# Key-feature gradient made transposed, 512 columns at a time, with its rows turned back by DMA

## The chip, the cores and the metric

The kernel runs on one core of a Trainium2 chip. The metric is the device time of one execution in microseconds (us). The kernel before has a median of 820.01 us over three runs (819.78 to 821.04).

The engines are called as the profile calls them: PE is the matrix engine (PEld its weight loads), DVE the vector engine, ACT the scalar engine, POOL the GpSimd engine, SP the sync engine, which here only issues DMAs. A matmul multiplies a stationary 128x128 operand (`lhsT`) with a moving operand of up to 512 columns and accumulates in PSUM, which has eight banks of 512 f32 values in each of 128 partitions. DVE and ACT bring results from PSUM to SBUF.

## The reference

The reference computes the output and all gradients of one transformer block: a layer norm, a linear attention with 32 heads of 20, a residual, a second layer norm, a gated MLP, a residual. Sizes: S = 2048 rows, D = 640, F = 1728, all in bf16. The part that matters here, cut:

```python
qkv = (x @ wqkv) ...                       # x is the normalised input, here xn
phi = lambda t: jnp.where(t > 0, t + 1, jnp.exp(t)) + 1e-6
pq, pk = phi(q), phi(k)
kv = jnp.einsum("bhsd,bhse->bhde", pk, v)
z = jnp.einsum("bhsd->bhd", pk)
num = jnp.einsum("bhqd,bhde->bhqe", pq, kv)
den = jnp.einsum("bhqd,bhd->bhq", pq, z)[..., None] + 1e-6
o = num / den
...
_out, _vjp = jax.vjp(_f, A_x, A_wqkv, A_wo, B_w1, B_w3, B_w2)
```

Backward through the key features: the gradient of `pk` is `xn @ gm + gz`, where `gm` (640x640) is the value weight times the gradient of `kv`, and `gz` (640 numbers) is the gradient of `z`. The gradient before the nonlinearity is `g_k = min(pk, 1) * (xn @ gm + gz)`. From it come the key part of the weight gradient, `xn^T @ g_k`, and, with `g_q` and `pk`, the gradient of `xn`: `[g_q, g_k, pk] @ wqT`, where `wqT` stacks the turned query weight, key weight and `gm`.

## The kernel before

The kernel is one program with its order written out by hand: each engine executes its instructions in the order of the source, waits are put in by the framework. It runs in stages: forward attention, forward and backward MLP, MLP weight gradients, the gradient of the second layer norm with the query side of the attention (`b_ghn`, `b_gr`, `b_gq`), then the stages that the change touches, then the big MLP weight gradients (`grad_job` over `blocks`, line 1335).

Rows are held as `[128 partitions, 16 tiles, 640]`, tile `t` being rows 128t to 128t+127. A turned tensor has the 640 features on partitions (five blocks of 128) and rows along the free side; `xnT[c]` holds 512 rows of turned `xn` (c = 0 to 3).

What the steps of the change and of the prediction touch, in order of time:

- **Last parts of the query side** (from line 1239). `part()` emits a piece of `q_parts` (line 1219), the matmuls that read `r_sb` and `g_h`. As each of its five outputs is complete, ACT copies it and SP turns it by DMA (line 1226, `QT`). In the same stretch SP issues the loads that turn `xn` (`load_xnT`, line 1242) and the weights (`load_wqT`, line 1299).
- **Jobs.** `wq_jobs` makes the weight gradients of q or k, in ten jobs (five blocks of 128 by two halves of 320 columns); a job is 16 matmuls of 320 columns into a PSUM tile of one bank (line 1335), one ACT copy to a place of `obs` (line 1339) and a DMA out (line 1341; POOL's queue for q, SP's for k). `fill(n)` emits n half jobs: it is how PE gets independent work between dependent pieces. `obs` holds 3200 columns, ten places of 320, which the jobs use in turn.
- **Squares.** `square` (line 1369) makes 128 rows of a 640x640 product into a tile of `d_acc`, which is `[128, 2, 512]` f32, two banks; there are three such tiles. Columns 0 to 379 lie in the first bank, 380 to 639 in the second. `unload` (line 1375) lets ACT copy the first bank's part and DVE the second's. Five squares make `dwoT`, five make `gm`, five make the value weight gradient, which also goes by way of `obs`: its five row blocks use columns 2560 on, then 0, 640, 1280 and 1920.
- **The key gradient** (loop from line 1436). A broadcast of `gz` over partitions is made first (lines 1426 to 1434). For each tile of 128 rows ten matmuls of 320 columns (line 1442) put `xn @ gm` into both banks of a `d_acc` tile; DVE adds `gz` (line 1445) and multiplies with `min(pk, 1)` (line 1446), `pk` rows being loaded by `load_pk`. After odd tiles below 13 comes `fill(1)`, after every third tile a square of the value gradient. All ten matmuls of a tile are issued before DVE reads the tile.
- **The gradient of x** (loop from line 1520). `e_gxn` issues 30 matmuls of 320 columns per tile (line 1505): five turned blocks of `g_q` and five of `g_k`, both brought by `e_T` (line 1498, a DMA transpose of 128x640), and five of the turned `pk` (`pkT`, loaded at line 1464). Then `ln_bwd` runs on ACT and DVE (lines 1143 to 1156), and SP writes the row tile out (line 1527). Twelve half jobs of the key weight gradient stand before the loop and two before every third tile of it. In the same loop SP loads the inputs of the last stage: `hnN` (line 1490) and the first blocks of the MLP gradients (line 1482).

The lines with which all this is ordered:

```python
def d_acc():
    return ps.tile([P, 2, 512], F32, name="dkv", bufs=3)
...
def unload(acc, out):
    for bank, (a, b) in enumerate(((0, SPLIT_D), (SPLIT_D, H))):
        (A.copy, V.tensor_copy)[bank](out=out[:, a * DH:b * DH], in_=acc[:, bank, 0:(b - a) * DH])
...
def fill(n):
    for _ in range(n):
        next(jobs, None)
```

An earlier product (`f2_wT`, lines 705 and 708) has the same shape as a square and the same split between ACT and DVE, but takes two PSUM tiles of one bank each.

Of the kernel before, what the change touches and what calls it, by code (L numbers as in the profile page):

```python
# [9 lines left out]
P = 128  # L10
BF16 = mybir.dt.bfloat16
F32 = mybir.dt.float32
ALU = mybir.AluOpType
# [42 lines left out]
def kernel(  # L56
# [19 lines left out]
    V, A, T, G, SY = nc.vector, nc.scalar, nc.tensor, nc.gpsimd, nc.sync  # L76
# [54 lines left out]
    class Stats:  # L131
# [150 lines left out]
    def two(ap):  # L282
        return ap.rearrange("p (j n) -> p j n", j=2)
# [1014 lines left out]
    def load_wqT(k):  # L1298
        dmaT(out=wqT[:, k * DT:(k + 1) * DT, :], in_=A_wqkv[:, k * D:(k + 1) * D])
# [11 lines left out]
    part(3)  # L1311
    load_xnT(1)
    part(4)
    part(4)
    part(20)
    load_xnT(2)
    V.reduce_sum(out=gz[:], in_=gz8[:], axis=AX.X)


# [42 lines left out]
    def d_acc():  # L1362
        return ps.tile([P, 2, 512], F32, name="dkv", bufs=3)

    def square(lhsT, rhs, i):

        acc = d_acc()
        for c, a, b, bank, off, first in SQ:
            T.matmul(acc[:, bank, off:off + (b - a) * DH], lhsT=lhsT[:, c, i * P:(i + 1) * P],  # L1369
                     rhs=rhs[:, c, a * DH:b * DH], start=first, stop=True, skip_group_check=True)  # L1370
        return acc
# [20 lines left out]
        if i > 1:  # L1392
            fill(1)
    br.release()
    bo.release()
    bv = pool("bv")
    pkT = bv.tile([P, DT, S], BF16, name="pkT")
    small = bv.tile([P, ST, D], BF16, name="small", tag="hnN")
    mN, gkv_b, gm = (small[:, n:n + DT] for n in (0, DT, 2 * DT))
    gzd = small[:, 3 * DT, :].rearrange("p (m q) -> p m q", q=P)  # L1400
    dx = pool("dx", "right")

    def load_pk(c):
        pkb[c] = dx.tile([P, 2, D], BF16, name="pkb", bufs=4)
        (dma if c < 4 else dmaG)(out=pkb[c][:], in_=pk_v[:, c * 2:(c + 1) * 2, :])

    gzb = dx.tile([P, D], F32, name="gzb")
    g_k = gqkv[1] = U1.tile([P, ST, D], BF16, name="g_k", tag="S0")
    load_pk(0)
    load_pk(1)  # L1410
    dma(out=mN, in_=m_v)
    dma(out=rows(dwoT_d), in_=dwoT[:])
    load_pk(2)
    load_pk(3)
    load_xnT(3)
    load_wqT(0)

    for i, (c, ms) in enumerate(SQ_BLOCKS):
        unload(square(wqT[:, 2 * DT:, :], gkvT, i), gm[:, i, :])
# [5 lines left out]
        if i == 0:  # L1425
            for m in range(DT):
                V.tensor_scalar(out=gzd[:, m, :], in0=ident[:], scalar1=gz[:, m:m + 1], scalar2=None, op0=ALU.mult)
        dmaT(out=wqT[:, 2 * DT:, i * P:(i + 1) * P], in_=gm[:, i, :])
    acc = d_acc()
    for m in range(DT):  # L1430
        T.matmul(acc[:, m // 4, m % 4 * P:(m % 4 + 1) * P], lhsT=ones[:], rhs=gzd[:, m, :], start=(m % 4 == 0),
                 stop=True, skip_group_check=True)
    for x, y, bank in ((0, 4 * P, 0), (4 * P, D, 1)):
        A.copy(out=gzb[:, x:y], in_=acc[:, bank, 0:y - x])

    for t in range(ST):
        c, i = divmod(t, TPC)
        u = t // 2
        acc = d_acc()
        for j in range(2):  # L1440
            for k in range(DT):
                T.matmul(acc[:, j, 0:HD], lhsT=xnT[c][:, k, i * P:(i + 1) * P], rhs=gm[:, k, j * HD:(j + 1) * HD],  # L1442
                         start=(k == 0), stop=(k == DT - 1))
        gp = dx.tile([P, D], F32, name="gp")
        V.tensor_tensor(out=two(gp[:]), in0=acc[:, :, 0:HD], in1=two(gzb[:]), op=ALU.add)
        V.scalar_tensor_tensor(out=g_k[:, t, :], in0=pkb[u][:, t % 2, :], scalar=1.0, in1=gp[:], op0=ALU.min,
                               op1=ALU.mult)
        if t % 2 and t < 13:
            fill(1)

        if t in (2, 5, 8, 11, 14):
            n = t // 3
            acc = square(mN, gkv_b, n)
            k = (4, 0, 1, 2, 3)[n]
            ob = obs[:, k * D:(k + 1) * D]
            unload(acc, ob)
            dmaG(out=out2S[:, n, 2 * D:3 * D], in_=ob)
        if t % 2 and u + 4 < 8:
            load_pk(u + 4)
        if t == 2:  # L1460
            load_wqT(1)
        if t in (6, 8, 10, 12):
            n = t // 2 - 3
            dmaT(out=pkT[:, :, n * W:(n + 1) * W], in_=pk_d[n * W:(n + 1) * W, :])
    for _ in jobs:
        pass
    dx.release()
# [1 line left out]


    ex = pool("ex", "right")
    hnN = bv.tile([P, ST, D], BF16, name="hnN")
    blocks = [(f0, min(f0 + NB, 2 * F)) for f0 in range(0, 2 * F, NB)]
    NB0 = 160

# [16 lines left out]
    gT = {}  # L1492

    def e_T(t, k):
        if k == 0:
            gT[t] = (ex.tile([P, 2 * DT, P], BF16, name="gT") if t % 3 == 2 else
                     bd[:, 2 * (t % 3):2 * (t % 3) + 2, :].rearrange("p c (k q) -> p (c k) q", q=P))
        dmaT(out=gT[t][:, k * DT:(k + 1) * DT, :], in_=gqkv[k][:, t, :])

    def e_gxn(t):  # L1500
        acc = ps.tile([P, 2, 512], F32, name="gxn", tag="gxn", bufs=2)
        for j in range(2):
            for k in range(15):
                g = gT[t][:, k, :] if k < 2 * DT else pkT[:, k - 2 * DT, t * P:(t + 1) * P]
                T.matmul(acc[:, j, 0:HD], lhsT=g, rhs=wqT[:, k, j * HD:(j + 1) * HD], start=(k == 0),  # L1505
                         stop=(k == 14))
        gx = scr[:, t % 2, :]
        ln_bwd(acc, t, xnN[:, t, :], ln1, gx, g_h[:, t, :], ex, scr[:, 2 + t % 2, :], scr[:, 4, :])()
        return gx
# [3 lines left out]
    njob = 2  # L1513
    jobs = wq_jobs((1,))
    scr = U1.tile([P, DT, D], BF16, name="scr", tag="W6")
    for t in range(3):
        for k in range(2):
            fill(2)
            e_T(t, k)
    for t in range(ST):  # L1520
        if t > 1 and t % 3 == 0:
            fill(2)
        gx = e_gxn(t)
        if t + 3 < ST:
            for k in range(2):
                e_T(t + 3, k)
        dma(out=out1S[:, t, :], in_=gx)
        if t in (2, 3, 5, 6):
            load_hnN((2, 3, 5, 6).index(t))
        if t in (7, 9, 12):  # L1530
            load_block(0, (t - 7) // 2 * NB0, (t - 5) // 2 * NB0 if t < 12 else NB)
        if t == 13:
            load_block(1)
    for _ in jobs:
        pass

# [32 lines left out]
            gw2_turn(i)  # L1569
    ps.release()  # L1570
    ex.release()
    bv.release()
    bl.release()
    U1.release()
# [31 lines left out]
```

## Time and profile before

| what | value |
|---|---|
| median of three runs | 820.01 us (819.78 to 821.04) |
| the profiled execution | 819.99 us; its span, first to last instruction, 817.9 us |
| PE | busy 811.8 us, 99% of the span |
| DVE, ACT, POOL | 55%, 40% and 16% |
| mean granted clock of PE | 1.000 |
| 560.7 to 579.1 us | half jobs, `dwoT`, `gm` |
| 579.1 to 609.5 us | the key gradient, with half jobs and squares |
| 609.5 to 624.7 us | rest of the query jobs, first key jobs |
| 624.7 to 698.6 us | the gradient of x, with the rest of the key jobs |
| 698.6 to 815.2 us | the MLP weight gradients |

Times in the profile are us from the start of the span unless marked ns. A group of instructions is given as line, engine, operation, output<-inputs, shape and count, then its busy time and the mean ns of one, then the idle time of its engine just ahead of it and what ended that. A matmul's shown duration is longer than its share of the stream: 30 matmuls of 512 columns in a row take 6.47 us, while each is shown with 379 ns.

### The profile page before, as it was taken

What the parts mean: (1) busy time and instruction counts of PE and PEld (TensorE: products, weight loads), DVE (VectorE), ACT (ScalarE), POOL (GpSimd) and SP (SyncE); (2) the same over time, 40 slices, a digit from 0 to 9 for tenths busy, and PEclk for the clock granted to TensorE, in tenths of its full rate; (3) what the DMA queues carried; (4) which work ended last, traced back from release to release, by engine and by line L of the source; (5) the groups of instructions that cost most, each with busy time, mean ns of one, the idle gap of its engine ahead of it and who ended that gap; (6) DMA issues with size and microseconds to landing.
All of it is one profiled execution on the core that took longest, in us unless ns stands there. A gap on an engine that the chain in (4) does not pass through costs nothing.

```text
span 817.9 us, 13715 instructions
## 1 busy us (share of the span) xinstructions
PE 811.8 (99%) x5261; PEld 501.6 (61%) x5292; DVE 452.7 (55%) x973; ACT 324.8 (40%) x609; POOL 131.8 (16%) x198
## 2 busy tenths in 40 slices
PE   9999999999999999999999999999999999999998
PEld 6777544555555555754577777777777777544444
DVE  7859997998898566300057777772781544200000
ACT  7856688665565666011222212222212334211111
POOL 2243333333222212100001111110220000000000
PEclk9999999999999999999999999999999999999999
DMA  9799899696485556999967877266997888979991
GB/s 268 201 243 287 198 270 319 196 242 174 126 211 157 165 175 168 230 238 243 260 176 182 214 198 196 58 113 142 252 206 158 182 193 158 240 179 233 218 242 37
DMA packets 335761, 162.46 MB, mean 199 GB/s; under 512 B 252304, under 2 KB 328944, under 8 KB 335696
## 3 DMA queue, kind: packets, MB, share of 16 engines
q1 hardware_dynamic: 291936, 120.68, 63.9%
q0 software_dynamic: 7328, 24.48, 9.2%
q10 hardware_dynamic: 36432, 16.42, 8.0%
q8 instruction: 41, 0.67, 0.4%
q14 instruction: 24, 0.20, 0.1%
HBM read 47.09 MB, written 53.43 MB: 123 GB/s over the span
## 4 chain that ended last, share of the span: by engine, by line
PE 98%; ACT 1%; DVE 1%; issue 0%; POOL 0%; ACTq 0%
PE mm L395 20%; PE job L1335 20%; PE ghn L1131 14%; PE gxn L1505 8%; PE gw L1086 7%; PE big L268 4%; PE o L913 4%; PE o L859 3%; PE gwo L1219 3%; PE macc L430 3%; PE gr L1188 3%; PE dkv L1442 3%; PE at L657 2%; PE mm L268 1%; PE dkv L1369 1%; PE gp L395 1%
## 5 line engine op out<-in xcount | busy, mean ns | idle before, releaser
L1335 PE MATMUL job<-gb,hnN 128*128 128x496 bf16 (+3 forms) x576 | 116.8, 366 | 0.0
L1131 PEld LDWEIGHTS <-ggb 128*128 128x128 bf16 x864 | 84.5, 98 | 33.0
L395 PE MATMUL mm<-pqT,w 128*128 128x512 bf16 x396 | 93.2, 379 | 0.5
L1335 PEld LDWEIGHTS <-hnN 128*128 128x128 bf16 x576 | 55.7, 98 | 61.1
L395 PEld LDWEIGHTS <-w 128*128 128x128 bf16 x540 | 52.5, 98 | 63.2 <-issue 0.6
L1339 ACT CAST obs<-job 128x496 bf16<-128x496 f32 (+4 forms) x56 | 28.5, 509 | 123.7 <-PE job L1335 123.7
L1131 PE MATMUL ghn<-w13a,ggb 128*128 128x320 bf16 x448 | 63.5, 299 | 0.0
L1146 DVE SCALAR_TENSOR_TENSOR wb<-gs,hnb 128x640 f32<-128x640 bf16 x16 | 13.2, 825 | 88.1 <-ACT gs L1143 88.1
L1131 PE MATMUL ghn<-w13b,ggb 128*128 128x320 bf16 x416 | 61.4, 299 | 0.0
L395 PE MATMUL mm<-g2T,w2T 128*128 128x512 bf16 x228 | 58.9, 379 | 0.6
L1086 PE MATMUL gw<-hb,g 128*128 128x512 bf16 (+2 forms) x316 | 58.4, 345 | 0.2
L1086 PEld LDWEIGHTS <-g 128*128 128x128 bf16 x320 | 31.3, 98 | 27.0
L420 ACT CAST ghh<-mm 128x512 bf16<-128x512 f32 x48 | 28.1, 585 | 47.6 <-PE mm L395 41.2
L1196 POOL TENSOR_TENSOR sz<-Zb,g_h 128x640 f32<-128x640 bf16 x16 | 20.2, 1261 | 163.8 <-DVE g_h L1197 163.8
L796 ACT ACTIVATE sig<-mm 128x512 bf16<-128x512 f32 x56 | 33.7, 602 | 25.5 <-PE mm L395 21.7
L1143 ACT ACTIVATE gs<-ghn 128x640 bf16<-128x640 f32 x16 | 11.2, 703 | 75.9 <-PE ghn L1131 66.1
L395 PEld LDWEIGHTS <-w2T 128*128 128x128 bf16 x260 | 25.4, 98 | 23.4
L268 PEld LDWEIGHTS <-pqT 128*128 128x128 bf16 x320 | 30.8, 98 | 13.4 <-ACT pqT L260 1.3
L268 PE MATMUL big<-wqkv,pqT 128*128 128x320 bf16 x250 | 38.4, 299 | 0.3
L1335 PEld LDWEIGHTS <-g 128*128 128x128 bf16 x320 | 31.0, 98 | 11.6
L832 DVE TENSOR_TENSOR gate<-gate,sig 128x1024 bf16<-128x1024 bf16 x28 | 19.3, 690 | 33.8 <-ACT gate L807 31.0
L1091 ACT CAST gw2o<-gw 128x512 bf16<-128x512 f32 (+2 forms) x20 | 10.4, 519 | 66.7 <-PE gw L1086 25.6
(217 smaller groups left out, 1391.8 us busy)
## 6 DMA issues: line engine op xcount, KB each, us to landing
hh_d<-hhT SPq DMA_DIRECT2D x24, 256.0 KB, 2.7
gg_d<-gate POOLq DMA_DIRECT2D x24, 256.0 KB, 4.2
gg_d<-ghh POOLq DMA_DIRECT2D x24, 256.0 KB, 3.9
ggb<-gg_d SPq DMA_DIRECT2D x6, 896.0 KB, 5.3
ggb<-gg_d ACTq DMA_DIRECT2D x6, 832.0 KB, 5.4
ggb<-gg_d SPq DMA_DIRECT2D x2, 1728.0 KB, 12.6
x_sb<-in_A_x_dram SPq DMA_DIRECT2D x4, 640.0 KB, 4.7
pk_d<-pk_all SPq DMA_DIRECT2D x4, 640.0 KB, 5.3
```

Of the source, the lines that this page charges most:

```text
L268: T.matmul(acc, lhsT=pqT[:, c, t * P:(t + 1) * P], rhs=wqkv[:, c, n0:n0 + HD], start=(c == 0), stop=(c == DT - 1))
L395: T.matmul(acc[:], lhsT=w[:, c, fc * P:(fc + 1) * P], rhs=rhs[:, c, :], start=(c == 0), stop=(c == DT - 1))
L420: A.copy(out=ghh[n // 2][:, n % 2, :], in_=acc[:])
L430: T.matmul(macc[m][j][:, 0:n], lhsT=pk_all[:, t, m * P:(m + 1) * P], rhs=x_ext[:, t, j * HD:j * HD + n], start=(t == 0), stop=(t == ST - 1))
L796: A.activation(sig[:, i, :], gp[:], AF.Sigmoid)
L859: T.matmul(accs[i, j][:, 0:HD], lhsT=hhT[c][:, fc, i * P:(i + 1) * P], rhs=w2[:, fc, j * HD:(j + 1) * HD], start=(first and fc == 0), stop ...
L913: T.matmul(o2["ps"][:, 0:HD], lhsT=hhT[c][:, fc, i * P:(i + 1) * P], rhs=w2[:, fc, j * HD:(j + 1) * HD], start=(fc == 0), stop=(fc == FT - 1))
L1086: T.matmul(acc[:, 0:fw], lhsT=g2[:, t, m * P:(m + 1) * P], rhs=hb[b][:, t, 0:fw], start=(t == 0), stop=(t == ST - 1))
L1131: T.matmul(acc[:, j, 0:HD], lhsT=ggb[t // 2][:, k, lo:lo + P], rhs=rhs[:, j * HD:(j + 1) * HD], start=(k == 0), stop=(k == NG - 1))
L1335: T.matmul(acc[:, 0:n], lhsT=lhs[:, t, m * P:(m + 1) * P], rhs=rhs(t), start=(t == 0), stop=(t == ST - 1))
L1339: A.copy(out=ob, in_=acc[:, 0:n])
L1505: T.matmul(acc[:, j, 0:HD], lhsT=g, rhs=wqT[:, k, j * HD:(j + 1) * HD], start=(k == 0), stop=(k == 14))
```

## The change

The key gradient is made turned. Instead of 16 row tiles of ten 320-column matmuls there are 20 pieces: for each of the four groups of 512 rows and each of the five blocks of 128 features, five matmuls with 512 moving columns. Within a group of 512 rows the pieces for feature blocks 0 and 1 share one `d_acc` tile, block 0 in its first bank and block 1 in its second, likewise blocks 2 and 3; block 4 has a tile of its own. Numbered through from 0 to 19, the pieces 1, 3, 6, 8, 11, 13, 16 and 18 are second halves of a tile. After each piece DVE makes `pm = min(pkT, 1)` (128x512, in SBUF), and then `g_kT = (piece + gz) * pm`, reading the piece's bank; `gz` is now a number per partition, so its broadcast goes. A half job follows each odd-numbered piece below 16, and a square of the value gradient the odd-numbered pieces 9 to 17.

`pkT` is needed for this and is loaded earlier, its first half into the room of `r_sb`; the loads of `pk` rows go. `e_gxn` takes the key part directly from `g_kT`, so `e_T` only turns `g_q`, five tiles ahead. The rows of `g_k`, which the key weight gradient needs, are brought by 20 DMA transposes of 128x512 (`k_turn`) during the gradient of x, and all ten key jobs stand behind that loop. `hnN` takes the room of `g_q` and is loaded at tiles 11 to 14, the first block at 11, 13 and 15, the second block after the loop. `load_wqT(0)` moves into the query side's last parts, `load_xnT(2)` behind the store of `dwoT`, the load of `mN` behind the turning of `gm`.

```diff
     load_xnT(1)
     part(4)
+    load_wqT(0)
     part(4)
     part(20)
-    load_xnT(2)
+    bo.release()
+    bv = pool("bv")
+    pkT = bv.tile([P, DT, S], BF16, name="pkT")
+
+    def load_pkT(c):
+        dmaT(out=pkT[:, :, c * W:(c + 1) * W], in_=pk_d[c * W:(c + 1) * W, :])
+
+    load_pkT(0)
+    load_pkT(1)
...
-    load_pk(0)
-    load_pk(1)
-    dma(out=mN, in_=m_v)
     dma(out=rows(dwoT_d), in_=dwoT[:])
-    load_pk(2)
-    load_pk(3)
-    load_xnT(3)
-    load_wqT(0)
+    load_xnT(2)
...
+    gT = {}
+
+    def e_T(t):
+        gT[t] = bd[:, t % DT, :].rearrange("p (k q) -> p k q", q=P)
+        dmaT(out=gT[t], in_=g_q[:, t, :])
+
+    mN = U1.tile([P, DT, D], BF16, name="mN", tag="W6")
+    load_pkT(2)
+    dma(out=mN[:], in_=m_v)
+    load_xnT(3)
+    load_pkT(3)
+    load_wqT(1)
+
+    for n in range(SC * DT):
+        c, d = divmod(n, DT)
+        cs = slice(c * W, (c + 1) * W)
+        if d % 2 == 0:
+            acc = d_acc()
+        for k in range(DT):
+            T.matmul(acc[:, d % 2, :], lhsT=gm[:, k, d * P:(d + 1) * P], rhs=xnT[c][:, k, :], start=(k == 0),
+                     stop=(k == DT - 1))
+        pm = dx.tile([P, W], BF16, name="pm", bufs=2)
+        V.tensor_scalar(out=pm[:], in0=pkT[:, d, cs], scalar1=1.0, scalar2=None, op0=ALU.min)
+        V.scalar_tensor_tensor(out=g_kT[:, d, cs], in0=acc[:, d % 2, :], scalar=gz[:, d:d + 1], in1=pm[:], op0=ALU.add,
                                op1=ALU.mult)
-        if t % 2 and t < 13:
+        if n % 2 and n < 16:
             fill(1)
+        if n > 8 and n % 2:
+            i = (n - 9) // 2
+            if i < DT:
+                sq = square(mN, gkv_b, i)
+                k = (4, 0, 1, 2, 3)[i]
+                ob = obs[:, k * D:(k + 1) * D]
+                unload(sq, ob)
+                dmaG(out=out2S[:, i, 2 * D:3 * D], in_=ob)
+    for t in range(DT):
+        e_T(t)
...
-    hnN = bv.tile([P, ST, D], BF16, name="hnN")
+    hnN = g_q
...
+    def k_turn(n):
+        c, d = divmod(n, DT)
+        dmaT(out=g_k[:, c * TPC:(c + 1) * TPC, d * P:(d + 1) * P], in_=g_kT[:, d, c * W:(c + 1) * W])
...
-                g = gT[t][:, k, :] if k < 2 * DT else pkT[:, k - 2 * DT, t * P:(t + 1) * P]
+                ts = slice(t * P, (t + 1) * P)
+                g = gT[t][:, k, :] if k < DT else g_kT[:, k - DT, ts] if k < 2 * DT else pkT[:, k - 2 * DT, ts]
...
-    for t in range(3):
-        for k in range(2):
-            fill(2)
-            e_T(t, k)
     for t in range(ST):
-        if t > 1 and t % 3 == 0:
-            fill(2)
         gx = e_gxn(t)
-        if t + 3 < ST:
-            for k in range(2):
-                e_T(t + 3, k)
+        if t + DT < ST:
+            e_T(t + DT)
+        for n in (2 * t, 2 * t + 1):
+            if n < SC * DT:
+                k_turn(n)
         dma(out=out1S[:, t, :], in_=gx)
-        if t in (2, 3, 5, 6):
-            load_hnN((2, 3, 5, 6).index(t))
...
+        if t > 10 and t < 15:
+            load_hnN(t - 11)
...
+    load_block(1)
     for _ in jobs:
         pass
```

More of the change, by code (lines that the diff above doesn't have):

```diff
@@ L1394 @@
     br.release()
[L1395 to L1407, printed above, removed]
+    bs = pool("bs")
+    g_kT = bs.tile([P, DT, S], BF16, name="g_kT")
+    dx = pool("dx")
+    gm, gkv_b = (dx.tile([P, DT, D], BF16, name=n) for n in ("gm", "gkv_b"))
     g_k = gqkv[1] = U1.tile([P, ST, D], BF16, name="g_k", tag="S0")
-    load_pk(0)
-    load_pk(1)
-    dma(out=mN, in_=m_v)
     dma(out=rows(dwoT_d), in_=dwoT[:])
-    load_pk(2)
-    load_pk(3)
-    load_xnT(3)
-    load_wqT(0)
+    load_xnT(2)
     for i, (c, ms) in enumerate(SQ_BLOCKS):
@@ L1424 @@
         fill(1)
-        if i == 0:
-            for m in range(DT):
-                V.tensor_scalar(out=gzd[:, m, :], in0=ident[:], scalar1=gz[:, m:m + 1], scalar2=None, op0=ALU.mult)
         dmaT(out=wqT[:, 2 * DT:, i * P:(i + 1) * P], in_=gm[:, i, :])
[L1429 to L1446, printed above, removed]
+    gT = {}
@@ L1447 @@
                                op1=ALU.mult)
-        if t % 2 and t < 13:
+        if n % 2 and n < 16:
             fill(1)
[L1451 to L1464, printed above, removed]
+        if n > 8 and n % 2:
[6 more added lines that the diff above has]
+                dmaG(out=out2S[:, i, 2 * D:3 * D], in_=ob)
@@ L1490, in load_hnN @@
         dma(out=hnN[:, i * TPC:(i + 1) * TPC, :], in_=hn_v[:, i * TPC:(i + 1) * TPC, :])
[L1492 to L1498, printed above, removed]
+    def k_turn(n):
+        c, d = divmod(n, DT)
+        dmaT(out=g_k[:, c * TPC:(c + 1) * TPC, d * P:(d + 1) * P], in_=g_kT[:, d, c * W:(c + 1) * W])
     def e_gxn(t):
@@ L1515 @@
     scr = U1.tile([P, DT, D], BF16, name="scr", tag="W6")
-    for t in range(3):
-        for k in range(2):
-            fill(2)
-            e_T(t, k)
     for t in range(ST):
-        if t > 1 and t % 3 == 0:
-            fill(2)
         gx = e_gxn(t)
-        if t + 3 < ST:
-            for k in range(2):
-                e_T(t + 3, k)
-        dma(out=out1S[:, t, :], in_=gx)
-        if t in (2, 3, 5, 6):
-            load_hnN((2, 3, 5, 6).index(t))
[L1530 to L1533, printed above, removed]
+        if t + DT < ST:
[3 more added lines that the diff above has]
+                k_turn(n)
+        dma(out=out1S[:, t, :], in_=gx)
+        if t > 10 and t < 15:
+            load_hnN(t - 11)
+        if t in (11, 13, 15):
+            load_block(0, (t - 11) // 2 * NB0, (t - 9) // 2 * NB0 if t < 15 else NB)
+    load_block(1)
     for _ in jobs:
@@ L1571 @@
     ex.release()
+    bs.release()
     bv.release()
```

## The prediction

> **What bounds the kernel now.** I read the page's engine line first, then the chain of waits, then the table by stage, then the instructions around the places that the change edits. The engine line and the table (busy time and count of PE, PEld, DVE, ACT and POOL, then clock, DMA share, GB/s; the four rows are the stages named above):
>
> ```profile
> PE 811.8 (99%) x5261; PEld 501.6 (61%) x5292; DVE 452.7 (55%) x973; ACT 324.8 (40%) x609; POOL 131.8 (16%) x198
> ...
> 560.70:579.14 18.44, 18.44 (x194) 14.83 (x193) 7.93 (x27) 7.09 (x16) 2.77 (x5) 1.00 0.81 224
> 579.14:609.50 30.36, 30.36 (x247) 22.41 (x245) 25.20 (x34) 4.64 (x11) 7.30 (x12) 1.00 1.19 208
> 609.50:624.70 15.20, 15.20 (x114) 10.94 (x113) 2.75 (x5) 2.55 (x6) 1.08 (x2) 1.00 0.91 192
> 624.70:698.60 73.90, 73.90 (x546) 53.16 (x544) 35.73 (x90) 27.38 (x50) 0.00 (x0) 1.00 0.83 172
> ```
>
> In every stage that the change touches PE is busy for the whole stage, at full clock. So nothing can be won by shortening a wait; only PE work taken away gains, and every new PE wait costs its full length. The chain, in order of time (start, length, what), with matmul counts:
>
> ```profile
> 6.46 0.98 PE k L268 x5
> ...
> 290.72 6.47 PE mm L395 x30
> ...
> 579.30 0.28 PE dkv L1431 x5
> 579.58 2.72 PE dkv L1442 x20
> 582.30 1.09 PE job L1335 x8
> ```
>
> It gives the prices on PE: 2.72/20 = 0.136 us for 320 columns, 6.47/30 = 0.216 for 512, 1.09 for a half job.
>
> The last view is what decides. A square fills two banks of one PSUM tile, ACT reads the first bank, DVE the second (timeline, then who waited, for line 1375; below it the same for line 708, where the banks are two tiles):
>
> ```profile
> 571.33 0.49 PE L1369 MATMUL dkv<-bd,wqT 128*128 128x140 bf16 x6
> ...
> 571.90 0.47 ACT L1375 CAST small<-dkv 128x380 bf16<-128x380 f32 x1 [0.99 <-PE dkv L1369]
> 572.41 0.43 DVE L1375 CAST small<-dkv 128x260 bf16<-128x260 f32 x1 [1.03 <-ACT small L1375]
> ...
>   DVE small L1375: 3.7, 4
>   DVE dwoT L1375: 2.4, 3
> ```
> ```profile
> 79.61 0.83 PE L705 MATMUL wt<-bd,wo 128*128 128x140 bf16 x12
> ...
> 79.99 0.91 ACT L708 CAST pkx<-wt 128x380 bf16<-128x380 f32 x2
> 80.14 0.76 DVE L708 CAST pkx<-wt 128x260 bf16<-128x260 f32 x2 [0.33 <-PE wt L705]
> ```
>
> With one tile DVE starts at 572.41, just after ACT ends (571.90 + 0.47), though it reads the other bank; and ACT starts only after the last of the six matmuls (571.33 + 0.49 = 571.82), though the last ones write the other bank. With two tiles ACT and DVE run side by side, and ACT starts at 79.99 while the matmuls into the other tile still run. So engines are ordered by tile, not by bank.
>
> **The change part by part.** *PE work.* Out: 160 matmuls of 320 columns, 160 x 0.136 = 21.76 us, and the broadcast of gz, 0.28. In: 100 of 512 columns, 100 x 0.216 = 21.57. Sum -0.47 us. Half jobs, squares and the 480 matmuls of the gradient of x keep count and shape.
>
> *The shared tile.* Within a tile the second piece's matmuls now stand behind DVE's read of the first. By the rows above PE must wait for that read. One wait: DVE starts 0.20 after a tile's stream ends (583.22 + 1.36 = 584.58; the add at line 1445 starts 584.78); the read of 512 columns is 0.69, on the line between the 260-column cast (0.428) and the 640-column operation at 1446 (0.825), bounds 0.48 (the 320-column add at line 664) and 0.825; PE restarts 0.05 after DVE ends (line 161 ends 95.76, PE 95.81). Together 0.94 (0.73 to 1.08). There are eight second pieces. Before 6, 8 and 16 a half job of 1.09 stands between and covers it: 0, and about 0.9 each if that cover were gone. Before 1, 3, 11, 13 nothing does: 4 x 0.94 = 3.8. Before 18 a square (0.34) covers a part, but DVE also has that square's second half to copy: 0.7. Before 11, DVE's half of a square (ACT 0.24 after it, 0.475, then DVE 0.42) and `pm` (0.33, from 0.378 for 640 columns at line 299) make the read 0.2 late, and 0.2 more falls on a square waiting for its tile at the end. Sum 4.9 (3.7 to 6.2).
>
> *obs.* The first value square goes to columns 2560 on, where query job 8 also writes. Before, that copy came long after the square's DMA; now it is due two pieces later. From the square's end: halves copied after 1.2, POOL's issue at 1.4, landing 5.0 later (line 1457: 3.3/5.0/6.8), so 6.4; the copy is due after pieces 10 and 11, two reads and a half job, at 4.6. ACT waits 1.8; behind it in its queue is the next square's first half, behind that DVE's second half, `pm` and the read of piece 12, and behind that PE at piece 13. 2.0 with the extra handoffs; 0.3 at 3.3, 5.3 at the slowest landing of that queue in this stretch (8.3). I take 2.0, from the row of the same DMA.
>
> *DVE, ACT, LN.* `pm` and reads are 20 x (0.33 + 0.69) = 20.4 us against 26.4 of lines 1445 and 1446; beyond the waits above, PE covers it. The layer norm backward now runs 16 tiles without pauses. ACT is idle 0.29 before line 1143 in each 4.08 us tile where no job stands between (690.49, 694.56), so it keeps pace: 0.
>
> *SP's queue.* `load_wqT(0)` stands before the last two turns of qp. Its issue takes 3.7 to 6.9 (line 1299), from 556.4, so the last turn is issued at 562.5 to 565.7 instead of 561.4 + 1.2 and lands 1.4 later; it is wanted at 565.8, covered by four half jobs: 0 (0 to 1.3). Then two `pkT` loads (3.6 each) to 570, dwoT's store at 571.4, `xnT(2)` to 576, five turns of gm (1.34 each, line 1428) to 583, `pkT(2)` to 586.5, `mN` landing 5.3 later at 592; the first value square wants it at 597: 0, 5 us to spare. `xnT(3)`, `pkT(3)`, `wqT(1)` (5.5) follow to 600, five `e_T` of 1.21 to 607; the gradient of x wants the first at 618: 0. The 2.6 MB of pk rows leave this stretch, four of those loads from POOL's queue. In the gradient of x SP issues per tile one `e_T` (1.21), two `k_turn` (4/5 of it each, bound 1.98 from line 1428) and a store (0.5), 3.6 (5.7) in 4.08; `e_T` is four tiles (16 us) ahead, which the bound of 1.6 per tile over ten tiles just uses up: 0. `hnN` and the blocks are issued later, but 20 half jobs (21.8) now follow the loop and cover them (landing 5 to 10): 0. The key jobs' stores wait behind the second block's 7.5 us issue; obs has ten places: 0.
>
> Sum: -0.47 + 4.9 + 2.0 = +6.4. On the profiled execution's 819.99, which is the median of 820.01 to 0.02, that is 826.4 us. Bounds: -0.47 + 3.7 + 0.3 = +3.5 and -0.47 + 6.2 + 5.3 + 1.3 = +12.3.
>
> **The rivals.** *Not slower: the second piece doesn't wait.* Place: pieces 1, 3, 11, 13, 18. If a matmul into the second bank is not ordered against a read of the first, 4.9 goes, and three tiles in turn hide most of the ACT wait; that leaves 0.7 to 1.8 at 5.0 landing and 0 at 4: 820.2, within the noise (changes under 0.2%, 1.64 us, can't be told from none here). It decides whether a read of a first piece and matmuls of its second overlap in time. For it: no row shows PE itself waiting this way. Against: both kinds of order above, ACT behind PE and DVE behind ACT across banks. The Trainium skill, "PSUM — Partial Sum Buffer", section "PSUM bank collisions raise a hardware error", says that accesses of two engines collide only within one bank and that different banks run clean; by that rule alone the chip needs no such wait and this rival would hold, while the rows show the order kept anyway.
>
> *PE's clock falls.* The loop would be the first place with idle PE time in it: 0.7 to 3 us, every few us. If the clock were halved for half of its 32 us of matmuls, +16: 842. Against: the granted clock is 1.00 in all stages, but none of them has such gaps. The Trainium skill, "TensorE: Matmul & The Clock Gate", section "A second HAM failure mode: psum-queue depth-cycling", says that short idles between groups of 512-column matmuls made the clock oscillate between half and full; no run here shows it.
>
> *Transfers late.* `xnT(3)` took 8.35 to issue in the old crowd instead of 3.6; if two loads ahead of `mN` do so, it lands 4 us late and PE stands at the first value square: 830.
>
> **How the numbers follow.** Forecast 0.78, between its bounds 823.5 and 832.3. No wait 0.14 (faster 0.02, same 0.08, slower 0.04). Clock 0.03. Late transfers 0.05. Faster 0.02, same 0.08, slower 0.90. The range 821 to 830.5 leaves out the low side of the no-wait case, the clock, and the far ends of the forecast, under 2 in 10.
>
> **What the profile after would show.** In the loop PE is idle about 7 us, ended by DVE's write of g_kT, in four waits near 0.94 and one near 3; none before pieces 6, 8, 16. ACT waits for an obs DMA near piece 11. The stage from 579 ends near 618. The gradient of x has no PE idle time, nor has the last stage. Wrong if PE is dense through the loop, if the idle time is ended by a DMA, or if the clock is below 1.00.

## The result and the profile after

The changed kernel takes 824.86 us (median of six runs, 824.38 to 826.14), beside 820.11 us for the kernel before on the same chip: a ratio of 1.0057, 95% interval 1.0046 to 1.0068. It is slower by 4.75 us. The forecast was 826.4 us, in a range of 821.0 to 830.5.

The engine line of the page, and the table by stage with the places where the stages now end (busy time and count of PE, PEld, DVE, ACT and POOL, then clock, DMA share, GB/s):

```profile
PE 813.5 (99%) x5227; PEld 495.8 (60%) x5227; DVE 445.0 (54%) x976; ACT 324.4 (39%) x607; POOL 128.7 (16%) x194
```
```profile
560.50:579.13 18.63, 18.63 (x196) 14.99 (x194) 7.11 (x22) 7.10 (x16) 2.76 (x5) 1.00 1.03 207
579.13:616.52 37.39, 32.73 (x196) 17.69 (x194) 20.41 (x45) 4.31 (x10) 5.40 (x10) 1.00 0.80 171
616.52:682.00 65.48, 65.48 (x484) 47.17 (x483) 36.48 (x92) 25.73 (x46) 0.00 (x0) 1.00 0.60 129
682.00:704.00 22.00, 22.00 (x163) 15.75 (x161) 2.56 (x7) 5.69 (x13) 0.00 (x0) 1.00 1.14 261
704.00:823.00 119.00, 116.26 (x575) 55.38 (x572) 0.00 (x0) 20.19 (x37) 0.00 (x0) 1.00 0.72 178
```

One stage has idle PE time that it didn't have: the new loop, 37.39 us of which PE is busy 32.73. The other stages of the change are full, at full clock. The engine line hides it: its busy share is still 99%, and its busy sum even rose by 1.7 us although there is less work. Of this rise 1.6 us lie between 20 us and the first half job (538.64 before, 540.26 after), where the two programs are equal and the trace of the kernel before shows 30 matmuls fewer (3446 and 3476): records that are missing. From the first half job to the last matmul's start the busy sum rises by 0.37 us (254.52 and 254.89), because the shown end of a matmul stream is modelled and each of the five broken streams carries a tail of 0.16 (five matmuls are shown with 1.24 us and are followed after 1.08). Work is therefore read from starts. Dense, the loop would take 31.9 us: 100 matmuls at 0.215, eight half jobs at 1.09, five squares at 0.34. It takes 5.5 us longer.

The list of PE's waits between 555 and 705 us (total, count, longest), and PE's timeline through the loop (start, length, what; in brackets the idle time ahead of it and what ended it):

```profile
PE dkv L1440 <- DVE g_kT L1444: 4.7, 5, 1.3
```
```profile
579.13 1.24 PE L1440 MATMUL dkv<-xnT,gm 128*128 128x512 bf16 x5
581.22 1.24 PE L1440 MATMUL dkv<-xnT,gm 128*128 128x512 bf16 x5 [0.84 <-DVE g_kT L1444]
582.29 1.25 PE L1344 MATMUL job<-g_q,g 128*128 128x320 bf16 x8
583.38 1.24 PE L1440 MATMUL dkv<-xnT,gm 128*128 128x512 bf16 x5
585.46 1.24 PE L1440 MATMUL dkv<-xnT,gm 128*128 128x512 bf16 x5 [0.84 <-DVE g_kT L1444]
...
597.69 1.24 PE L1440 MATMUL dkv<-xnT,gm 128*128 128x512 bf16 x5
599.93 1.24 PE L1440 MATMUL dkv<-xnT,gm 128*128 128x512 bf16 x5 [1.00 <-DVE g_kT L1444]
...
602.43 1.24 PE L1440 MATMUL dkv<-xnT,gm 128*128 128x512 bf16 x5
605.00 1.24 PE L1440 MATMUL dkv<-xnT,gm 128*128 128x512 bf16 x5 [1.33 <-DVE g_kT L1444]
...
613.23 0.49 PE L1378 MATMUL dkv<-gkv_b,mN 128*128 128x140 bf16 x6
614.37 2.32 PE L1440 MATMUL dkv<-xnT,gm 128*128 128x512 bf16 x10 [0.65 <-DVE g_kT L1444]
```

There are five waits, all ended by DVE's write of `g_kT`, at the second pieces 1, 3, 11, 13 and 18, and none at 6, 8 and 16, where a half job stands between. From start to start they lose 1.01, 1.00, 1.16, 1.49 and 0.80 us (first: 581.22 - 579.13 = 2.09, less the 1.08 of five matmuls), 5.46 in all; the list shows 4.7, since each shown wait begins only behind a tail of 0.16. The order around the first of them, on both engines:

```profile
579.13 1.24 PE L1440 MATMUL dkv<-xnT,gm 128*128 128x512 bf16 x5
...
580.41 0.75 DVE L1444 SCALAR_TENSOR_TENSOR g_kT<-dkv,gz,pm 128x512 bf16<-128x512 f32 x1 [0.95 <-PE dkv L1440]
...
581.22 1.24 PE L1440 MATMUL dkv<-xnT,gm 128*128 128x512 bf16 x5 [0.84 <-DVE g_kT L1444]
```

DVE starts 0.20 after the stream ends (579.13 + 1.08 = 580.21), reads for 0.75, and PE starts 0.06 after that, in the other bank of the same tile.

The longest wait, before piece 13, contains the obs conflict. The timeline of POOL, ACT and DVE from the first value square's store on:

```profile
599.12 0.54 POOL L1455 DMA_DIRECT2D out_dram<-obs  x1 [3.55 <-DVE pm L1443]
...
602.63 0.42 ACT L1348 CAST obs<-job 128x320 bf16<-128x320 f32 x1 [4.26 <-PE dkv L1378]
602.95 0.48 ACT L1384 CAST obs<-dkv 128x380 bf16<-128x380 f32 x1
...
603.46 0.43 DVE L1384 CAST obs<-dkv 128x260 bf16<-128x260 f32 x1 [1.50 <-ACT obs L1384]
603.81 0.28 DVE L1443 TENSOR_SCALAR pm<-pkT 128x512 bf16<-128x512 bf16 x1
...
604.20 0.75 DVE L1444 SCALAR_TENSOR_TENSOR g_kT<-dkv,gz,pm 128x512 bf16<-128x512 f32 x1
```

The store was issued at 599.12 and landed at 602.53. Query job 8's copy was due 0.2 after the job's matmuls end (602.10), at 602.30, and starts at 602.63. So ACT waited 0.33, and the chain behind it (the square's first half, its second half, `pm`, the read of piece 12) is late by as much. The profile puts the end of this wait down to PE's square at line 1378, which the job's copy doesn't read and whose shown end (602.10 + 0.49) lies close to the landing; the run with other places in `obs`, below, shows that the copy starts 0.20 after its job when the store isn't in its way.

The whole difference in the profile, from the first half job (560.50 before, 560.49 after) to the last matmul's start (815.02 and 820.04), is +5.03 us: 5.46 of waits less 0.43 of PE work.

### The profile page after: what moved, and what is told of

Read it like the earlier page. It is cut to its first block, busy times and chain, and to the rows that moved or that the text cites. A ratio compares the mean times of both kernels' runs of the same rounds, so it can differ in the third digit from the quotient of the medians.

```text
span 823.0 us, 13581 instructions
## 1 busy us (share of the span) xinstructions
PE 813.5 (99%) x5227; PEld 495.8 (60%) x5227; DVE 445.0 (54%) x976; ACT 324.4 (39%) x607; POOL 128.7 (16%) x194
## 4 chain that ended last, share of the span: by engine, by line
PE 96%; DVE 1%; ACT 1%; DMA 1%; SPq 0%; issue 0%; POOL 0%; DVEq 0%; ACTq 0%
PE mm L395 20%; PE job L1344 19%; PE ghn L1131 14%; PE gxn L1495 8%; PE gw L1086 7%; PE big L268 4%; PE o L913 4%; PE o L859 3%; PE gwo L1219 3%; PE macc L430 3%; PE gr L1188 3%; PE dkv L1440 2%; PE at L657 2%; PE mm L268 1%; DMA wqkv<-in_A_wqkv_dram 1%; PE dkv L1378 1%
## 5 line engine op out<-in xcount | busy, mean ns | idle before, releaser
L1344 PE MATMUL job<-gb,g_q 128*128 128x496 bf16 (+3 forms) x576 | 116.8, 366 | 0.0
L1344 PEld LDWEIGHTS <-g_q 128*128 128x128 bf16 x576 | 55.8, 98 | 61.0
L1146 DVE SCALAR_TENSOR_TENSOR wb<-gs,hnb 128x640 f32<-128x640 bf16 x16 | 13.2, 825 | 88.1 <-ACT gs L1143 88.1
```

The costliest lines, as they stand in the source:

```text
L1344: T.matmul(acc[:, 0:n], lhsT=lhs[:, t, m * P:(m + 1) * P], rhs=rhs(t), start=(t == 0), stop=(t == ST - 1))
```

## The experiments

### Is a tile the unit of order? The kernel before, with its reads split

Two edits of the kernel *before*, whose loop has no wait. Both split DVE's addition of `gz` into its two banks. The first issues the read of the first bank ahead of the second bank's matmuls, the second behind them; the rest is equal.

```diff
+        gp = dx.tile([P, D], F32, name="gp")
         for j in range(2):
             for k in range(DT):
                 T.matmul(acc[:, j, 0:HD], ...)
-        gp = dx.tile([P, D], F32, name="gp")
-        V.tensor_tensor(out=two(gp[:]), in0=acc[:, :, 0:HD], in1=two(gzb[:]), op=ALU.add)
+            V.tensor_tensor(out=gp[:, j * HD:(j + 1) * HD], in0=acc[:, j, 0:HD], in1=gzb[:, j * HD:(j + 1) * HD], op=ALU.add)
```

> The kernel before, whose key gradient takes both banks of one tile per 128 rows. DVE's addition of gz is cut into two halves of 320 columns, and the half for the first bank is issued ahead of the matmuls into the second bank. Theory (engines are ordered by tile): PE waits in each of the 16 tiles for the first half's read, 0.20 + 0.48 + 0.05 = 0.73 us, +11.7 us: 832 (830 to 834). Rival (ordered by bank, or no order of PE behind a read): 820 to 822, for DVE's additional 16 x 0.14 us of work.

Measured: 838.61 us, ratio 1.0218 (1.0202 to 1.0235). The list of waits, and the timeline of the first tile:

```profile
PE dkv L1443 <- DVE gp L1445: 16.3, 16, 1.4
```
```profile
579.25 0.84 PE L1443 MATMUL dkv<-small,xnT 128*128 128x320 bf16 x5
580.20 0.49 DVE L1445 TENSOR_TENSOR gp<-dkv,gzb 128x320 f32<-128x320 f32 x1 [1.09 <-PE dkv L1443]
580.74 1.52 PE L1443 MATMUL dkv<-small,xnT 128*128 128x320 bf16 x10 [0.65 <-DVE gp L1445]
```

Sixteen tiles, sixteen waits. The cost is larger than expected, since the waits are not all of the first one's size: where no half job stands between two tiles, DVE is still at the tile before (second half 0.49, multiply 0.82) when the first half could be read, and the wait grows from 0.65 to as much as 1.43.

The control, with both reads behind both banks' matmuls:

```diff
-        V.tensor_tensor(out=two(gp[:]), in0=acc[:, :, 0:HD], in1=two(gzb[:]), op=ALU.add)
+        for j in range(2):
+            V.tensor_tensor(out=gp[:, j * HD:(j + 1) * HD], in0=acc[:, j, 0:HD], in1=gzb[:, j * HD:(j + 1) * HD], op=ALU.add)
```

> Control of the run with the read inside: the same two halves of 320 columns, both issued behind the matmuls of both banks. All theories: no PE wait of this kind; 820 to 822 for DVE's additional 2.2 us of work, which makes DVE about as long as PE in this loop (30.7 against 30.0 us). Only the order of the source differs between the two runs.

Measured: 819.77 us, ratio 0.9985 (0.9964 to 1.0005), no PE wait in the loop. So neither the split nor the added instruction costs; the place of the read in the program does. A matmul into one bank waits for an earlier-issued read of the other bank of its tile.

### The changed kernel with a tile for every piece

```diff
-        if d % 2 == 0:
-            acc = d_acc()
+        acc = ps.tile([P, W], F32, name="gkT", tag="dkv", bufs=3)
...
-            T.matmul(acc[:, d % 2, :], ...)
+            T.matmul(acc[:], ...)
...
-        V.scalar_tensor_tensor(out=g_kT[:, d, cs], in0=acc[:, d % 2, :], ...)
+        V.scalar_tensor_tensor(out=g_kT[:, d, cs], in0=acc[:], ...)
```

> The changed kernel, with a PSUM tile of its own for each of the 20 pieces (three buffers as before, the same matmuls, reads, half jobs and squares in the same order). Theory (a piece's matmuls wait because the read of the piece ahead is in the same tile): the five PE waits of the loop (5.5 us) go, the loop over pieces shrinks from 37.4 to about 32.0 us, and the time is that of the kernel before less the matmul overhead, 819.6 (819.3 to 820.6). Rival (the waits come from DVE being slow, from the number of buffers, or from the 512-column form): the waits stay, 824 to 825; with three one-bank buffers instead of three two-bank ones a lack of buffers would even lengthen them. It also prices all the other parts of the change together, since they are all kept: if the time is 819.6 they cost nothing.

Measured: 822.18 us, ratio 1.0024 (1.0013 to 1.0035). All five waits are gone, and 2.7 us of the loss; but two other waits came, and the expectation of 819.6 (to 820.6) was missed by 2.6. The list of waits, and the timeline around them (ACT, then PE):

```profile
PE dkv L1378 <- DVE obs L1384: 1.1, 1, 1.1
PE gkT L1439 <- DVE g_kT L1443: 0.6, 1, 0.6
```
```profile
602.66 0.43 ACT L1348 CAST obs<-job 128x320 bf16<-128x320 f32 x1 [6.04 <-DMA out_dram<-obs]
...
603.98 0.49 PE L1378 MATMUL dkv<-gkv_b,mN 128*128 128x140 bf16 x6 [1.05 <-DVE obs L1384]
```

Here ACT does stand for a long time at the first square's store (issued 597.38, landed 602.57): the loop runs ahead by what the tiles no longer cost, so job 8's copy is due earlier while the store lands at the same moment. The reason seemed to be the obs conflict; the other possible one was that three tiles of one bank hold less than three of two. The next pair tells these apart.

### The obs conflict alone

The value squares go to the places 0, 1, 2, 3, 0 of `obs` (counted here in blocks of 640 columns) instead of 4, 0, 1, 2, 3, so that none uses a place whose other user comes within a few us.

```diff
-                k = (4, 0, 1, 2, 3)[i]
+                k = (0, 1, 2, 3, 0)[i]
```

With a tile for every piece:

> The kernel with a tile of its own for every piece, and beside that the value squares staged in the places 0, 1, 2, 3, 0 of obs (before 4, 0, 1, 2, 3), so that no copy waits for a transfer issued a few us before. If the 2.2 us that this arrangement still lost over before came from ACT waiting 6.0 us for the first square's transfer (and from the square's and the piece's waits behind it, 1.1 and 0.6), the loop has no PE wait left and the time is 819.3 to 820.3. If it came from having only three one-bank buffers where there were three two-bank ones, the waits for DVE stay and the time is 821.5 to 822.5.

Measured: 820.03 us, ratio 1.0000 (0.9987 to 1.0013), 2.15 us under the same kernel without this line (2.0 by the two ratios, each taken to the kernel before on the same chip). The loop has no PE wait, and ACT's copy starts when its job is done (timeline of ACT):

```profile
599.55 0.42 ACT L1348 CAST obs<-job 128x320 bf16<-128x320 f32 x1 [2.73 <-PE job L1344]
599.92 0.47 ACT L1384 CAST obs<-dkv 128x380 bf16<-128x380 f32 x1
```

So the second cost was the obs conflict, not the number of banks. From the first half job (560.91) to the last matmul's start (815.00) this profile has 254.09 us, the kernel before 254.52: the 0.43 us of PE work that the change takes away are there, but the medians don't resolve them.

With the changed kernel's shared tiles:

> The changed kernel with its shared tiles, only the places of the value squares in obs changed to 0, 1, 2, 3, 0. If the shared tile is the cause and the obs conflict costs little once the tiles delay the loop, only the wait before piece 13 shrinks (1.33 to about 1.0) and the one before piece 11 stays: 824.3 to 824.7, that is 0.2 to 0.5 under the changed kernel's 824.86. If obs has the larger part, two of the five waits go: 822.5 to 823.

Measured: 825.13 us, ratio 1.0052 (1.0034 to 1.0070), where the changed kernel has 1.0057 (1.0046 to 1.0068). Piece 13's wait shrinks from 1.33 to 1.05 and equals piece 11's, ACT's copy starts at 602.18, the span falls from 823.0 to 822.6; in the medians nothing can be seen, and the expected 824.3 to 824.7 was not met. With shared tiles the obs conflict is worth some 0.3 us, because the tiles' own waits have delayed job 8 to nearly the moment of the landing.

### Shared tiles without the wait: the order of the program

Two ways to keep the two-bank tile and lose the wait. The first puts a half job between the two pieces of each tile:

```diff
-        if n % 2 and n < 16:
+        if d in (0, 2):
             fill(1)
```

> The changed kernel with its shared tiles kept, and its eight half jobs moved: one after each first piece of a shared tile (feature blocks 0 and 2) instead of after the odd-numbered pieces. Theory: each wait (1.0 us) is now covered by a half job of 1.09 us, so no PE wait is left and the time is 819.6 to 820.2, though the tiles are still shared. Rival (PE lacks buffers, or DVE is the bound of the loop): 824 to 825, with the waits at other pieces.

Measured: 820.33 us, ratio 1.0002 (0.9992 to 1.0012), 0.1 above the expected range. The loop takes 32.1 us and has no PE wait; ACT still waits at `obs` (until 602.69), with nothing behind it that PE wants in time. The profiled execution has one wait elsewhere, ahead of the loop (timeline of PE):

```profile
567.45 0.78 PE L1395 MATMUL gkvT<-tri,woT 128*128 128x140 bf16 x10 [1.86 <-DMA tri<-tri]
```

This is the last turn of qp, which this time took 5.0 us from issue to landing instead of the 2.6 that it took before and in the changed kernel's profile.

The second leaves the half jobs where the changed kernel has them, takes the new places in `obs`, and issues `pm` and the read of a first piece behind the second piece's matmuls:

```diff
-        pm = ...
-        V.tensor_scalar(out=pm[:], in0=pkT[:, d, cs], ...)
-        V.scalar_tensor_tensor(out=g_kT[:, d, cs], in0=acc[:, d % 2, :], scalar=gz[:, d:d + 1], ...)
+        for e in (d - 1, d) if d % 2 else (d,) if d == DT - 1 else ():
+            pm = ...
+            V.tensor_scalar(out=pm[:], in0=pkT[:, e, cs], ...)
+            V.scalar_tensor_tensor(out=g_kT[:, e, cs], in0=acc[:, e % 2, :], scalar=gz[:, e:e + 1], ...)
```

> Shared tiles as in the changed kernel and the new obs places; the multiply and the read of a first piece are issued behind the second piece's matmuls, so DVE reads both banks after both are written. If PE waits only because the read stands between the two pieces in the program, no wait is left in the loop, and the time is 819.3 to 820.5; DVE then has two reads in a row (2 x 1.0 us) where it had one, which three tiles cover. If the sharing of a tile costs by itself, whatever the order: 822 to 825.

Measured: 820.19 us, ratio 0.9991 (0.9974 to 1.0007), no PE wait in the loop. The shared tile costs nothing by itself: only a read that stands in the program between two writes of one tile does.

### The half job between, with the queue of loads changed too

To see whether the change's 0.47 us can be had as time, and whether the late turn of qp comes from the load put ahead of it:

```diff
-    load_wqT(0)
...
     load_pkT(0)
     load_pkT(1)
+    load_wqT(0)
...
-        if n % 2 and n < 16:
+        if d in (0, 2):
             fill(1)
...
-                k = (4, 0, 1, 2, 3)[i]
+                k = (0, 1, 2, 3, 0)[i]
```

> The version with a half job between the two pieces of every tile, the new obs places, and the load of wqT's query rows moved behind the last two turns of qp and the first two loads of pkT. If the 0 to 2 us by which that version's executions spread came from the last turn landing late behind this load, the spread goes and the time is 819.4 to 819.8, that is 0.2 to 0.6 under before, the 0.47 us of PE work that the change takes away. If the loads now pushed back are late in turn (m_v at the first value square), 820.5 to 822.

Measured: 820.48 us, ratio 0.9999 (0.9988 to 1.0011), runs from 819.42 to 821.89. The expectation failed: the spread is as wide as before the edit. In the profile the turn of qp is in time, but SP's later issues moved by some 3.5 us against the changed kernel's, `mN` lands at 595.22 instead of 592.04, and PE waits 0.27 us for it. Whether the load ahead of the turns makes them late was not settled: of the profiles of kernels that keep it there, two show PE waiting for the turn (1.86 with the half job between, 0.6 with every piece read three times), and six don't. No version here is measurably faster than the kernel before.

### The wait doubled: what a longer read does

Every piece is read twice, then three times, by the same instruction with the same inputs.

```diff
+        for _ in range(2):
             V.scalar_tensor_tensor(out=g_kT[:, d, cs], in0=acc[:, d % 2, :], ...)
```

> The changed kernel with DVE's read of each piece done twice (the same result written twice), 0.67 us more per piece. Theory: each second piece waits 0.67 longer; pieces 1, 3, 11, 13 and 18 give 5 x 0.67 = 3.4, and the half job no longer covers pieces 6 and 8 (0.95 + 0.67 - 1.09 = 0.5 each) nor, in part, 16 and the squares: about +6 us, 830.5 (829 to 832). DVE has then 20 x 1.6 = 32 us of work in a loop of 43 us and is not the bound. If the waits had nothing to do with the read's length: 825.

Measured: 834.29 us, ratio 1.0172 (1.0156 to 1.0188), 9.4 over the changed kernel and above the expected 829 to 832. All eight second pieces now wait, 13.0 us in place of 4.7; the three that half jobs cover wait 1.1 to 1.3 each, more than expected, because DVE's two reads of the piece before are in the way too. That is 8.3. The rest is the clock. The table by stretches around the end of the loop, and PE's timeline there:

```profile
620.00:622.00 2.00, 0.77 (x9) 0.46 (x7) 1.85 (x4) 0.47 (x1) 0.00 (x0) 1.00 0.11 41
622.00:624.00 2.00, 1.17 (x5) 0.48 (x5) 1.29 (x3) 0.00 (x0) 0.54 (x1) 0.95 0.00 0
624.00:626.00 2.00, 2.00 (x6) 0.76 (x5) 1.70 (x3) 0.00 (x0) 0.00 (x0) 0.50 0.23 82
626.00:628.00 2.00, 2.00 (x11) 1.20 (x10) 1.50 (x2) 0.00 (x0) 0.00 (x0) 0.70 0.00 0
```
```profile
618.12 2.32 PE L1440 MATMUL dkv<-xnT,gm 128*128 128x512 bf16 x9 [1.13 <-DVE g_kT L1445]
...
622.83 3.52 PE L1440 MATMUL dkv<-xnT,gm 128*128 128x512 bf16 x10 [2.06 <-DVE g_kT L1445]
626.14 1.37 PE L1496 MATMUL gxn<-wqT,bd 128*128 128x320 bf16 x5
627.35 0.84 PE L1496 MATMUL gxn<-wqT,g_kT 128*128 128x320 bf16 x5
```

After a wait of 2.06 us the granted clock falls to 0.50 for a stretch. The ten and five matmuls from 622.83 take until 627.35, 4.52 us, where ten at 0.215 and five at 0.136 would take 2.83: 1.7 us lost. 8.3 + 1.7 = 10.0, of the 10.1 us between the two spans (833.1 and 823.0). Of the four executions, two have a mean clock of 0.998 (835.15, which is the profiled one, and 835.0 us) and two of 1.000 (833.58 and 833.42): the same program loses the clock in some executions and not in others.

> As with every piece read twice, but three times (the result stays the same). That kernel's eight waits of 1.1 to 2.1 grow by one read, 0.77, each: 834.3 + 8 x 0.77 = 840.5, if the clock does no worse than there (half speed in one stretch of some 4 us after the last wait of 2.06, about 1.7 us lost). If half speed follows an idle time of 2 us or more between short runs of matmuls, as it did there, most pieces now run at half speed: up to 8 x 1.1 more, 845 to 850, and the granted clock in the loop is well under 1.00.

Measured, in one execution: 856.68 us, span 854.9, mean clock 0.982. The eight waits are 22.5 us. PE's timeline around the longest wait, and the table for the stretches on either side:

```profile
608.01 2.32 PE L1440 MATMUL dkv<-xnT,gm 128*128 128x512 bf16 x10 [1.86 <-DVE g_kT L1445]
...
611.66 1.24 PE L1440 MATMUL dkv<-xnT,gm 128*128 128x512 bf16 x5
617.25 2.29 PE L1440 MATMUL dkv<-xnT,gm 128*128 128x512 bf16 x5 [4.35 <-DVE g_kT L1445]
619.34 2.34 PE L1344 MATMUL job<-g_q,g 128*128 128x320 bf16 x8
```
```profile
608.00:612.00 4.00, 3.99 (x26) 2.32 (x26) 2.69 (x6) 0.22 (x1) 0.00 (x0) 1.00 0.07 25
612.00:617.00 5.00, 0.90 (x5) 0.29 (x3) 4.75 (x8) 0.26 (x1) 0.54 (x1) 0.81 0.09 33
617.00:621.00 4.00, 3.75 (x12) 1.64 (x12) 1.78 (x4) 0.00 (x0) 0.00 (x0) 0.50 0.00 0
```

The clock theory's direction holds and its size was too small. Seven of the eight waits are 2.42 us or longer, and the matmuls after each of the seven run slow, wholly or in part; after the eighth, 1.86, ten matmuls take 2.32 as at full clock. The span is 31.9 us above the changed kernel's, of which the waits are 17.8 (22.5 - 4.7). A further 0.6 is one wait for the turn of qp, as in the profile with the half job between. Nearly all of the remaining 13.5 us are slower matmuls: between 584 and 650 us nine stretches of 3.41 us run at a clock of 0.50, PE is shown busy for 26.4 us of them, and half of that is 13.2 (an estimate).

## Why the prediction was right, and where a size was off

**The verdict and its mechanism were right.** The forecast was slower, by waits of PE in the new loop that DVE's reads end. The profile shows them at the five places named and at no other.

**PE work, -0.47.** Measured -0.43 by landmarks. The price of a 512-column matmul, taken from a stream of the forward pass, held: 0.215 here.

**The shared tile, 4.9.** One wait was put at 0.94, as 0.20 + 0.69 + 0.05; measured 1.01, as 0.20 + 0.75 + 0.06. The interpolated read of 512 columns was 0.06 short, the two handoffs were right to 0.01. Piece 11 was forecast 0.2 longer than the others, 1.14, and lost 1.16. Piece 18 was forecast at 0.7, and lost 0.80. A last 0.2 for a square waiting for its tile did not occur. With piece 13 at piece 11's value, as it is without the obs conflict, the five are 1.01 + 1.00 + 1.16 + 1.16 + 0.80 = 5.13. That the order goes by tile was read from how ACT and DVE alternate in `unload`; no row showed PE in that place. The pair of edits of the kernel before confirmed it (16 waits against none), and the read put behind the second piece showed that order and not sharing is the cause. The Trainium skill, "PSUM — Partial Sum Buffer", section "PSUM bank collisions raise a hardware error", says that accesses to different banks run clean and so gives no reason to wait; the trace shows the wait all the same, 5.13 us of it, since it is the program's semaphores that PE waits for.

**The obs conflict, 2.0.** This is the term that was mis-sized: it measured 0.33, and the wait before piece 13, forecast near 3, lost 1.49. The mechanism came as told (ACT's copy of job 8 behind the first square's store, then the square, `pm`, the read, piece 13), and so did two of its three times: POOL issued 1.43 after the square's end at 597.69 (1.4 forecast), and the copy was due 4.6 after it (4.6 forecast). Wrong was the landing: 3.4 us, not the 5.0 of the median row; 0.33 is the low end of the bounds, which had been worked out with a landing of 3.3. In the kernels with own tiles, own tiles and new places, the new places alone, and the changed kernel, the square's store was issued at 597.38, 597.58, 599.00 and 599.12, and landed at 602.57, 602.56, 602.45 and 602.53. There it is the moment of landing that stays, not the duration: 0.3 us ahead of the weight load then in progress (`load_wqT(1)`: 602.85, 602.85, 602.75 and 602.81). With the read moved back it is the same, later (issued 598.10, landed 602.84, the load 603.14); with the half job between it is not (597.70, 602.59, the load 605.08). In the last version, with the queue of loads changed, it is 597.09 and 602.20. What sets that moment was not tested. Of the total's miss, 826.4 against 824.86, this term explains 1.67, and the read's length and the rest take back some 0.2.

**One cost covers the other.** Without the tiles' waits job 8's copy comes earlier, the landing does not, and the conflict costs more: the rival without waits put it at 0.7 to 1.8 us, and with own tiles it measured 2.15 in the medians (2.0 by the ratios). So own tiles alone leave the kernel slower than before (1.0024), and with the new places too it is at 1.0000. The half job between the pieces gets by without the new places (1.0002): ACT waits at `obs` there too, but PE does not notice.

**What was put at zero.** `mN` landed at 592.04 (592 forecast) and was wanted at 597.36 (597). The turns of gm and the loads after them were issued as forecast to within 1 us. The gradient of x has no PE idle time in 65.48 us, though SP needs 4.55 us per tile there instead of 3.6: a `k_turn` takes 1.25 us to issue, not 4/5 of the 1.21 for 640 columns. Stores of that stretch are late enough for DVE to wait 7.7 us in five places (`scr`, line 1156), and PE notices none of it. The last block loads landed at 695.3 and 702.9, covered by the 20 half jobs. The late turn of qp, bounded by 1.3, does not appear in the changed kernel's profile; with the half job between, one execution shows it with 1.86, outside that bound.

**The rivals.** *No wait* fell with the trace. *Transfers late* did not occur in the changed kernel. *The clock falls* did not occur either (1.00 in every stage). The runs with longer reads show that gaps in this loop can bring it about; how far the changed kernel is from that stands in the last section.

## What to carry to other kernels

In a loop that PE fills, ask of every accumulator that holds two independent results whether a read of the first is issued before the writes of the second; if so, each tile costs a whole handoff and read (here 1.0 us), and giving each result its own tile, moving the read back or putting other matmuls between removes it for nothing. Look for the next conflict in the version that has the first one removed: a reused staging place that cost 0.3 us behind the waits cost 2 us without them. Don't carry a DMA's duration over from another place without a range: in seven kernels the same store landed between 602.20 and 602.84, though it was issued anywhere from 597.09 to 599.12, so here the moment was the better guide than the duration; why was not tested.

## What the runs showed that was not expected

- **The clock fell after stretches of 3.41 us in which PE did little; the length of one wait is only a rough guide.** In the loop with longer reads, waits of up to 1.86 us left the granted clock at 1.00, and all seven waits of 2.42 us and more were followed by slower matmuls. But of two nearly equal waits, one (2.06, ending at 622.83) was followed by half clock and the other (2.07, ending at 605.19) was not. What tells them apart is how much PE did in a fixed stretch. In each profile that has two or more changes of the clock on record, they lie whole multiples of 3.41 us apart. Cut along that grid, the loop with two reads shows (columns as in the table by stage):

```profile
603.31:606.73 3.42, 1.49 (x8) 0.83 (x9) 2.15 (x5) 0.00 (x0) 0.54 (x1) 1.00 0.82 176
606.73:610.14 3.41, 2.19 (x17) 1.25 (x16) 2.81 (x6) 0.80 (x2) 1.08 (x2) 1.00 0.29 64
620.38:623.79 3.41, 1.35 (x12) 0.74 (x10) 2.79 (x6) 0.47 (x1) 0.38 (x1) 1.00 0.00 0
623.79:627.21 3.42, 3.42 (x11) 1.37 (x10) 2.49 (x5) 0.00 (x0) 0.16 (x1) 0.50 0.13 48
```

The stretch with 1.49 us of busy PE is followed by full clock, the one with 1.35 by half. With every piece read three times, the seven stretches at full clock with 0.53 to 1.31 us are each followed by half clock, and the one with 1.56 is not; in the kernel before with the read inside, the barest stretch has 1.52 and full clock follows. So in these profiles the border lies between 1.35 and 1.49 us of shown busy time in 3.41; no run was made to test it by itself. In the changed kernel, whose longest wait is 1.33 shown and 1.49 lost, even the barest 3.41 us (601.58 to 604.99) have 2.09. The Trainium skill, "TensorE: Matmul & The Clock Gate", section "HAM oscillation — how this bites in real kernels", gives as a rule that PE should have no idle gaps over about 3.4 us; in this loop the clock fell after 2.06 and 2.42 us, so the measured gaps are shorter than that rule's.
- **A turn by DMA costs SP nearly the same for 512 columns as for 640.** From 619 us on the first ones take 1.22 to 1.25 us of issue and 2.5 to 2.6 us to landing, for 128x512 (`k_turn`) as for 128x640 (`e_T`).
- **Some small stores land together with a large load.** Under the loads that turn `xn`, `pk` and the weights, POOL's 80 and 160 KB stores landed 1.9 to 6.5 us after their issue in one and the same loop, three of them within 0.3 us of the landing of the load in progress (595.02 and 595.30, 599.65 and 599.43, 602.53 and 602.81).
